# First batch's partial sums between two feed-forward turns: from DRAM to SBUF, with the second turn's inputs in the activations' ring

## The chip, the cores and the metric

The kernel runs on one core of a Trainium2 chip. The metric is the device time of one execution in microseconds (us). Engines are named as in the profile: PE (matrix products) with its weight loads PEld, DVE (vector), ACT (scalar), POOL (GpSimd), and SP, which here only issues DMAs, in order, each after its waits.

## The reference

```
x    = concat_heads(softmax(mask(q k^T / 8)) v)   # 8 batches, 8 heads, 576 tokens, 64 wide; mask by blocks of 64
h    = (x^T @ U @ V)^T                            # mixes the tokens, rank 32
u    = x + h                                      # [8, 576, 512]
out  = u + max(u @ w_ch1, 0) @ w_ch2              # 512 -> 2048 -> 512
```

All arrays are float32; `U`, `V`, `w_ch1` and `w_ch2` are float64 and are turned into float32 pairs on the chip.

## The kernel before, in words

The work is written as tasks, each with an engine, an estimated duration, a priority, the buffers that it reads, writes or only holds, and a delay until a DMA lands. `Plan.issue` then plays the tasks through with these estimates and issues on each engine the ready task with the lowest priority number. That game fixes the order of the instructions on every engine before the kernel is built; on the chip each engine keeps to its order and waits where an operand is late. A change of a task's waits or of its place moves the order of everything that the game comes to afterwards. In that game two tasks that use the SBUF port which DVE and POOL share (flag `port`, and every POOL task) never run together.

Attention goes head by head (64 heads, priorities 0 to 64,000). For each head: q and k are split into a high and a low part (POOL lines 894, 895), copied into the lower 64 partitions by two DMAs (lines 897, 898, `q<-q`, `k<-k`), multiplied (PE lines 944, or 948 and 949), reduced to a maximum (DVE 962), exponentiated (ACT 973), normalised (DVE 989, 990; POOL 999), transposed (PE 1032; its copies are ACT 1009 and DVE 1051 into `ph`, `pl`) and applied to v (PE 1091). `mix` (1116 to 1160) makes the input u of the feed-forward part and stores it in DRAM (`u_d`).

The feed-forward part fills PE's gaps: its products have priorities of 1e6 and more. The first 1024 of the 2048 hidden units are done by `ffn_chunk`, for 16 chunks of 288 tokens (two for each batch). One chunk: u is loaded into `ur` (two sets of four tiles, chunk c uses set c mod 2), split into `uh` (ACT 445) and `ul` (POOL 447, four instructions in a row), multiplied by the first weights into a PSUM bank (PE 465), read out with a maximum against zero into `hh` (ACT 470) and its rest `hl` (DVE 473), multiplied by the second weights (PE 488), added to u (DVE 494, into `ot`) and stored (SP 499, into `o_d`). All this has two PSUM banks, `banks_f` (`bf_90`, `bf_91`). `hh` and `hl` are rings of 10 tiles, taken in turn by `take`.

While the weights of the first half still arrive (their pieces pass through `st` and `z`: SP 372 and 387, ACT 353 and 360, DVE 331, 332, 337, 345, POOL 361), the two chunks of batch 0 are done in two turns: turn 0 with hidden units 0 to 511, turn 1 with 512 to 1023.

```
    for n in range(2):
        for c in range(CPB):
            ffn_chunk(c, lambda: wa, wab, range(n * FH, (n + 1) * FH), n)
    for c in range(CPB, NCHUNK):
        ffn_chunk(c, lambda: wa, wab)
```

Before, turn 0 stores u plus its products in `o_d`; turn 1 loads u from `u_d` again, splits it, and then loads the sums from `o_d` over it (SP 452). The last 1024 hidden units follow as block products of seven instead of eight (PE 659), after attention has ended.

Of the kernel before, what the change touches and what calls it, by code (L numbers as in the profile page):

```python
# [24 lines left out]
KC = DM // P  # L25
FC = HF // P
T = 288
# [26 lines left out]
NEAR, DL = 130, 3000  # L54
# [83 lines left out]
class Plan:  # L138
# [8 lines left out]
    def add(self, engine, ns, prio, fn, reads=(), writes=(), hold=(), after=0, port=False):  # L147

        n = len(self.tasks)
        deps = set()  # L150
        for b in reads:
            deps.update(b.writers)
            b.readers.append(n)
        for b in hold:
            deps.update(b.readers, b.writers)
        for b in writes:
            deps.update(b.readers, b.writers)
            b.writers, b.readers = [n], []
        deps.discard(n)
        slots = {b for b in (*reads, *writes) if b.pool is not None}  # L160
        for b in slots:
            b.users += 1
        self.tasks.append((engine, ns, prio, fn, deps, after, slots, port or engine == "POOL"))
# [76 lines left out]
def _act(n, sbuf=False):  # L240
    return (93 if sbuf else 52) + 0.833 * n


def _dve(n):
    return 69 + 1.042 * n


def _pe(*ns, m=()):

    m = [*m, *[P] * len(ns)][1 : len(ns)] + [P]  # L250
    return sum(max(0.85 * w, n * COL) for n, w in zip(ns, m))
# [3 lines left out]
def attention_then_mixer(  # L255
# [10 lines left out]
    nc = tc.nc  # L266
# [8 lines left out]
    add = plan.add  # L275

    def f32(ap):
        return ap.bitcast(F32)
# [15 lines left out]
    u_d = [dram.tile([P, KC, S], F32, name=f"u_d{b}") for b in range(B)]  # L294
    o_d = [dram.tile([P, KC, S], F32, name=f"o_d{b}") for b in range(B)]
    u_s = [[Buf().split(CPB) for _ in range(NPAIR)] for _ in range(B)]
    o_s = [[Buf() for _ in range(KC)] for _ in range(NCHUNK)]
# [10 lines left out]
    def take(r, name):  # L308
        n = used[name] = used.get(name, -1) + 1
        return r[n % len(r)]  # L310
# [112 lines left out]
    hh_r, hl_r = ([Buf() for _ in range(FC + 2)] for _ in range(2))  # L423
    ot_t = fp.tile([P, 3, T], F32, name="ot")
    ot_r = [Buf(ot_t[:, n, :]) for n in range(3)]
# [5 lines left out]
    def ffn_chunk(c, w, wb, fr=range(FC), turn=0):  # L431

        b, o = c // CPB, (c % CPB) * T
        banks, done = banks_f if c < NCHUNK - 1 else Part(banks_f, banks_f), ffn_done[c]
        E, F = -1.0, 1e6 + (1300 + 300 * c if turn else 1000 * c)
        ur = ur_r[c % 2]
        for k in range(KC):
            if b > 0 or turn:
                add(
                    "SP", 630, E, lambda k=k: nc.sync.dma_start(out=ur[k].ap, in_=u_d[b][:, k, o : o + T]),  # L440
                    u_s[b][k].parts, [ur[k]], after=DL,
                )
        for k in range(KC):
            uh, ul = uh_r[k], ul_r[k]
            add("ACT", _act(T, True), E, lambda u=ur[k], h=uh: nc.scalar.copy(h.ap, u.ap), [ur[k]], [uh])
            add(
                "POOL", 780, E, lambda u=ur[k], h=uh, l=ul: nc.gpsimd.tensor_sub(l.ap, u.ap, f32(h.ap)),  # L447
                [ur[k], uh], [ul],
            )
            if turn:  # L450
                add(
                    "SP", 630, E, lambda k=k: nc.sync.dma_start(out=ur[k].ap, in_=o_d[b][:, k, o : o + T]),
                    [o_s[c][k]], [ur[k]], after=DL,
                )
        hs = {}
        for f in fr:
            ps = Buf(pool=banks)
            fs = slice(f * P, (f + 1) * P)
            ops = [(wn, k, m) for wn, m in (("w1h", uh_r), ("w1l", uh_r), ("w1h", ul_r)) for k in range(KC)]
            for g in range(0, len(ops), GM):  # L460

                def products(g=g, ps=ps, fs=fs, ops=ops):
                    for i in range(g, g + GM):
                        wn, k, m = ops[i]
                        nc.tensor.matmul(ps[:, :T], w()[wn][:, k, fs], m[k].ap, start=(i == 0), stop=(i == len(ops) - 1))  # L465

                sub = ops[g : g + GM]
                add("PE", _pe(*[T] * GM), F, products, [m[k] for _, k, m in sub] + [wb["w1"][f * P // CW][k] for _, k, _ in sub], [ps])
            th, tl = take(hh_r, "hh"), take(hl_r, "hl")
            add("ACT", _act(T), E, lambda ps=ps, th=th: nc.scalar.activation(th.ap, ps[:, :T], AF.Relu), [ps], [th])  # L470
            add(
                "DVE", _dve(T), E,
                lambda ps=ps, th=th, tl=tl: nc.vector.scalar_tensor_tensor(  # L473
                    out=tl.ap, in0=ps[:, :T], scalar=0.0, in1=f32(th.ap), op0=ALU.max, op1=ALU.subtract
                ),
                [ps, th], [tl],
            )
            hs[f] = (th, tl)
        for m in range(KC):
            ps = Buf(pool=banks)  # L480
            ms = slice(m * P, (m + 1) * P)
            ops = [(wn, f, x) for f in fr for wn, x in (("w2h", 0), ("w2l", 0), ("w2h", 1))]
            for g in range(0, len(ops), GM):

                def products(g=g, ps=ps, ms=ms, ops=ops):
                    for i in range(g, g + GM):
                        wn, f, x = ops[i]
                        nc.tensor.matmul(ps[:, :T], w()[wn][:, f, ms], hs[f][x].ap, start=(i == 0), stop=(i == len(ops) - 1))  # L488

                sub = ops[g : g + GM]  # L490
                add("PE", _pe(*[T] * GM), F, products, [hs[f][x] for _, f, x in sub] + [wb["w2"][f] for _, f, _ in sub], [ps])
            ot = take(ot_r, "ot")
            add(
                "DVE", _dve(T), E, lambda ps=ps, ot=ot, m=m: nc.vector.tensor_add(ot.ap, ps[:, :T], ur[m].ap),
                [ps, ur[m]], [ot],
            )
            done.writers.append(len(plan.tasks) - 1)
            add(
                "SP", 630, E, lambda ot=ot, m=m: nc.sync.dma_start(out=o_d[b][:, m, o : o + T], in_=ot.ap), [ot],
                [o_s[c][m]], after=DL,  # L500
            )
# [308 lines left out]
    for r in raw_r:  # L810
# [3 lines left out]
        for x, fill in ((qi, 1.0), (ki, NEG)):  # L814
            nc.gpsimd.affine_select(
                out=x[:, :, 1, :], in_=x[:, :, 1, :], pattern=[[-1, 4], [0, 64]], compare_op=ALU.not_equal,
# [390 lines left out]
# [5 lines that stand above are left out]
# [40 lines left out]
```

## Time and profile before

| | |
|---|---|
| time, median of 3 runs | 1182.98 us (1182.54 to 1184.93) |
| the profiled execution's own time | 1186.81 us |
| its span in the profile | 1185.0 us |
| PE busy | 1165.8 us, 98% |
| DVE, ACT, POOL busy | 937.3, 775.9, 451.3 us |
| DMA | 122.69 MB, mean 104 GB/s |
| mean granted TensorE clock | 0.998 |

The span runs from the first to the last recorded instruction. PE has the same matrix products to do in any order, so its idle time and the time at a lowered clock are what an order can win or lose.

### The profile page before, as it was taken

The page shows a single profiled execution, that of the slowest core. Times are in us where ns is not written, and L with a number is a line of the kernel's source. Part 1 is how long each engine was busy: PE and PEld are TensorE (multiplying, and loading weights), DVE is VectorE, ACT ScalarE, POOL GpSimd, SP SyncE. Part 2 cuts the span into 40 slices and gives each one's busy share as a digit, 9 for nine tenths or more (in the row PEclk, how much of TensorE's full clock was granted, in tenths as well). Part 3 has the DMA queues.
Part 4 walks back from the last instruction along what each step waited for, and adds up shares of the span by engine and source line. Part 5 has one row for each costly group of instructions (what it writes and reads, how often), then busy time and mean ns, then how long its engine had stood idle before and what let it go on. Part 6 is the DMA issues. An engine that isn't in the chain of part 4 may idle for free.

```text
span 1185.0 us, 25201 instructions
## 1 busy us (share of the span) xinstructions
PE 1165.8 (98%) x8988; PEld 1133.4 (96%) x8988; DVE 937.3 (79%) x2008; ACT 775.9 (65%) x1924; POOL 451.3 (38%) x582
## 2 busy tenths in 40 slices
PE   9989899999999999999999999999999999999998
PEld 7778899999999999999999999999999999999998
DVE  6898888877787878787877587326989889889887
ACT  7888787889888888898887342114544444444443
POOL 5656767576767676766674112110000000000000
PEclk9999999999999999999999999999999999999999
DMA  5455555444434434444331434211232132142121
GB/s 139 146 150 154 136 170 151 118 120 112 115 112 113 112 105 112 121 113 106 110 102 51 138 115 133 75 50 52 61 121 65 57 120 70 52 121 66 56 81 41
DMA packets 75868, 122.69 MB, mean 104 GB/s; under 512 B 8928, under 2 KB 52960, under 8 KB 75744
## 3 DMA queue, kind: packets, MB, share of 16 engines
q1 hardware_dynamic: 75744, 121.09, 35.6%
q8 instruction: 71, 1.16, 0.4%
q14 instruction: 53, 0.43, 0.1%
HBM read 76.23 MB, written 29.49 MB: 89 GB/s over the span
## 4 chain that ended last, share of the span: by engine, by line
PE 77%; DVE 10%; ACT 8%; issue 3%; DMA 2%; SPq 0%; POOL 0%; ACTq 0%; DVEq 0%; POOLq 0%
PE bb L659 30%; PE bf L465 10%; PE bf L488 10%; PE ba L1032 6%; PE ba L1091 5%; PE bg L488 4%; PE bg L465 4%; ACT p L973 3%; DVE mx L962 2%; PE ba L949 2%; PE ba L948 2%; DVE pl L1051 1%; PE bw L948 1%; ACT ph L1009 1%; PE ba L1116 1%
## 5 line engine op out<-in xcount | busy, mean ns | idle before, releaser
L999 POOL TENSOR_SCALAR p<-p,rv 128x192 f32<-128x192 f32 (+4 forms) x320 | 172.1, 553 | 157.6 <-DVE rv L990 84.5
L659 PE MATMUL bb<-hh,w1l 128*128 128x288 f32 x704 | 170.1, 295 | 0.0
L659 PE MATMUL bb<-hh,w1h 128*128 128x288 f32 x704 | 169.4, 295 | 0.0
L1051 DVE TENSOR_TENSOR pl<-ba,ph 128x512 fp32r<-128x512 f32 x216 | 113.8, 551 | 18.3 <-ACT ph L1009 16.0
L973 ACT ACTIVATE p<-ba,mx 128x448 f32<-128x448 f32 (+2 forms) x248 | 115.0, 466 | 15.4 <-DVE mx L962 11.8
L1032 PE MATMUL ba<-ident,p 128*128 128x128 f32 x768 | 123.0, 275 | 2.0 <-POOL p L999 0.7
L659 PE MATMUL bb<-hl,w1h 128*128 128x288 f32 x576 | 123.0, 295 | 0.1
L659 PEld LDWEIGHTS bb<-hh,w1l 128*128 128x128 f32 x704 | 123.0, 190 | 0.0
L659 PEld LDWEIGHTS bb<-hh,w1h 128*128 128x128 f32 x704 | 121.9, 188 | 0.0
L488 PE MATMUL bf<-hh,w2h 128*128 128x288 f32 x384 | 119.0, 310 | 2.3 <-DVE hl L473 2.3
L488 PE MATMUL bf<-hl,w2h 128*128 128x288 f32 x384 | 113.8, 296 | 0.0
L488 PE MATMUL bf<-hh,w2l 128*128 128x288 f32 x384 | 113.0, 294 | 0.0
L447 POOL TENSOR_TENSOR ul<-ur,uh 128x288 fp32r<-128x288 f32 x72 | 61.6, 884 | 127.1 <-PE bf L465 80.8
L1009 ACT CAST ph<-ba 128x512 fp32r<-128x512 f32 x216 | 99.0, 492 | 10.8 <-PE ba L1032 9.6
L613 ACT CAST hh<-hb 128x576 fp32r<-128x576 f32 x98 | 65.9, 672 | 60.5 <-PE bb L659 59.3
L962 DVE TENSOR_REDUCE mx<-ba 128x1 f32<-128x448 f32 (+3 forms) x248 | 95.2, 406 | 11.2 <-PE ba L949 8.6
L1032 PEld LDWEIGHTS ba<-ident,p 128*128 128x128 f32 x768 | 90.0, 141 | 7.5 <-POOL p L999 2.7
L659 PEld LDWEIGHTS bb<-hl,w1h 128*128 128x128 f32 x576 | 91.9, 188 | 0.4 <-DVE hl L614 0.4
L1091 PE MATMUL ba<-ph,vs 128*128 128x256 f32 (+3 forms) x432 | 90.4, 263 | 0.0
L465 PE MATMUL bf<-uh,w1l 128*128 128x288 f32 x392 | 82.1, 305 | 0.0
L894 POOL TENSOR_TENSOR q<-raw,q 64x576 fp32r<-64x576 f32 x52 | 73.8, 1419 | 7.7 <-issue 5.4
L895 POOL TENSOR_TENSOR k<-raw,k 64x576 fp32r<-64x576 f32 x52 | 75.1, 1445 | 2.2 <-POOL p L999 0.5
(172 smaller groups left out, 3363.4 us busy)
## 6 DMA issues: line engine op xcount, KB each, us to landing
raw<-in_qk_dram SPq DMA_DIRECT2D x63, 288.0 KB, 3.9
st<-in_w_dram SPq DMA_DIRECT2D x32, 512.0 KB, 4.1
o_d<-ot SPq DMA_DIRECT2D x72, 144.0 KB, 1.8
vr<-in_v_dram SPq DMA_DIRECT2D x32, 320.0 KB, 3.7
ur<-u_d SPq DMA_DIRECT2D x64, 144.0 KB, 2.5
whole<-o_d SPq DMA_DIRECT2D x32, 288.0 KB, 3.2
out_dram<-whole SPq DMA_DIRECT2D x32, 288.0 KB, 2.2
ur<-u_d SPq DMA_DIRECT2D x30, 288.0 KB, 3.2
```

What stands on the lines that cost most here:

```text
L465: nc.tensor.matmul(ps[:, :T], w()[wn][:, k, fs], m[k].ap, start=(i == 0), stop=(i == len(ops) - 1))
L488: nc.tensor.matmul(ps[:, :T], w()[wn][:, f, ms], hs[f][x].ap, start=(i == 0), stop=(i == len(ops) - 1))
L659: nc.tensor.matmul(bank[:, i, :T], x()[:, w(k)], p.ap[:, k, :], start=first and n == 0, stop=last and n == len(ops) - 1)
L894: add("POOL", 1380, pr, lambda: nc.gpsimd.tensor_sub(q1[top], raw[top, 0:S], f32(q2[top])), [raw, q2], [q1])
L895: add("POOL", 1380, pr, lambda: nc.gpsimd.tensor_sub(k2[top], raw[top, S : 2 * S], f32(k1[top])), [raw, k1], [k2])
L962: lambda i=i, at=at: nc.vector.tensor_reduce(out=mx[: P if i else 64, i : i + 1], in_=view(i, at), op=ALU.max, axis=AX.XY if wide else AX. ...
L973: nc.scalar.activation(out.rearrange("p (j k) -> p j k", j=2) if wide else out, view(i, at), AF.Exp, bias=mx[:rows, i : i + 1], accum_out= ...
L999: lambda x=x, rows=rows, i=i: nc.gpsimd.tensor_scalar(out=x, in0=x, scalar1=rv[:rows, i : i + 1], scalar2=1.0, op0=ALU.mult, op1=ALU.mult),
L1009: add("ACT", _act(n), pr, lambda: nc.scalar.copy(out(), inp()), reads, writes)
L1032: nc.tensor.transpose(out=bank[:, a : a + P], in_=pt_r[i][h % PB[i]][:, j * P : (j + 1) * P], identity=perm.ap)
L1051: "DVE", _dve(m), pr, lambda: nc.vector.tensor_sub(pl[:, low], bank[:, :m], f32(ph[:, low])), [bank, bh], [bl]
L1091: nc.tensor.matmul(bank[0 : c.stop, a:n], vs[:, j, c], x[:, _at(g, j)], start=(i == 0), stop=(i == len(ops) - 1))
```

## The change

Turn 0's sums are added into `ur` itself and stay there; nothing goes to `o_d`. Turn 1 takes four tiles of the `hh` ring for its inputs, loads u into them (as bits of the same size), splits from there, adds its products to `ur`, and stores the end sums as before. So eight stores (`o_d<-ot`) and eight loads (`ur<-o_d`) of 144 KB go; the eight loads of u in turn 1 stay, with another target and other waits. Eight tiles more are taken from the ring of `hh`, none from that of `hl`.

```
         ur = ur_r[c % 2]
+
+        us = [take(hh_r, "hh") for _ in range(KC)] if turn else ur
         for k in range(KC):
+            u, at = us[k], (lambda u=us[k]: f32(u.ap) if turn else u.ap)
             if b > 0 or turn:
                 add(
-                    "SP", 630, E, lambda k=k: nc.sync.dma_start(out=ur[k].ap, in_=u_d[b][:, k, o : o + T]),
-                    u_s[b][k].parts, [ur[k]], after=DL,
+                    "SP", 630, E, lambda k=k, at=at: nc.sync.dma_start(out=at(), in_=u_d[b][:, k, o : o + T]),
+                    u_s[b][k].parts, [u], after=DL,
                 )
-        for k in range(KC):
             uh, ul = uh_r[k], ul_r[k]
-            add("ACT", _act(T, True), E, lambda u=ur[k], h=uh: nc.scalar.copy(h.ap, u.ap), [ur[k]], [uh])
-            add(
-                "POOL", 780, E, lambda u=ur[k], h=uh, l=ul: nc.gpsimd.tensor_sub(l.ap, u.ap, f32(h.ap)),
-                [ur[k], uh], [ul],
-            )
-            if turn:
-                add(
-                    "SP", 630, E, lambda k=k: nc.sync.dma_start(out=ur[k].ap, in_=o_d[b][:, k, o : o + T]),
-                    [o_s[c][k]], [ur[k]], after=DL,
-                )
+            add("ACT", _act(T, True), E, lambda at=at, h=uh: nc.scalar.copy(h.ap, at()), [u], [uh])
+            add(
+                "POOL", 780, E, lambda at=at, h=uh, l=ul: nc.gpsimd.tensor_sub(l.ap, at(), f32(h.ap)), [u, uh], [ul],
+            )
...
-            ot = take(ot_r, "ot")
+            ot = ur[m] if len(fr) < FC and not turn else take(ot_r, "ot")
...
+            if ot is ur[m]:
+                continue
```

The order changes from early in turn 0 on. Three places, which the prediction calls A, B and C; line numbers after the change are lower by two to four behind the edit (465, 473, 488, 494 are 461, 469, 484, 490).

**Place A, end of turn 0's first layer for chunk 0.** On PE, before, two products of `mix` stand between the last first-layer product (into `bf_91`) and the first second-layer product:

```order
L465 MATMUL bf_91<-ul_113,w1h_212 128x288
L1145 MATMUL ba_96<-v_183,t_0_178 128x288
L1145 MATMUL ba_97<-v_183,t_0_178 128x288
L488 MATMUL bf_90<-hh,w2h_214 128x288
L488 MATMUL bf_90<-hh,w2l_215 128x288
L488 MATMUL bf_90<-hl,w2h_214 128x288
```

On PE after the change, at the same place:

```order
L461 MATMUL bf_91<-ul_113,w1h_212 128x288
L484 MATMUL bf_90<-hh,w2h_214 128x288
L484 MATMUL bf_90<-hh,w2l_215 128x288
L484 MATMUL bf_90<-hl,w2h_214 128x288
L484 MATMUL bf_90<-hh,w2h_214 128x288
L484 MATMUL bf_90<-hh,w2l_215 128x288
L484 MATMUL bf_90<-hl,w2h_214 128x288
L484 MATMUL bf_91<-hh,w2h_214 128x288
```

The two products of `mix` have moved behind twelve second-layer products, and six of these write `bf_91` right behind the six on `bf_90`. On DVE, before, the reading out of the two banks (`hl`) at the same place:

```order
L1136 TENSOR_TENSOR t_0_178<-tz_179,t_0_178 32x128
L989 TENSOR_REDUCE rv_167<-ss_144 128x2
L990 RECIPROCAL rv_167<-rv_167 128x2
L337 SCALAR_TENSOR_TENSOR z_102<-st_100,z_102 128x512
L473 SCALAR_TENSOR_TENSOR hl<-bf_90,hh 128x288
L345 SCALAR_TENSOR_TENSOR z_102<-st_100,z_102 128x512
L1150 TENSOR_TENSOR ut_181<-ba_96,xt_174 128x288
L473 SCALAR_TENSOR_TENSOR hl<-bf_91,hh 128x288
```

On DVE after the change:

```order
L987 TENSOR_REDUCE rv_167<-ss_144 128x2
L988 RECIPROCAL rv_167<-rv_167 128x2
L469 SCALAR_TENSOR_TENSOR hl<-bf_90,hh 128x288
L987 TENSOR_REDUCE rv_167<-ss_144 128x3
L988 RECIPROCAL rv_167<-rv_167 128x3
L1134 TENSOR_TENSOR t_0_178<-tz_179,t_0_178 32x128
L345 SCALAR_TENSOR_TENSOR z_102<-st_100,z_102 128x512
L469 SCALAR_TENSOR_TENSOR hl<-bf_91,hh 128x288
```

Line 345, a piece of the weights, still stands ahead of the second `hl`, and now a second pair of `rv` and line 1136's successor (1134) do as well.

**Place B, the DMAs of the next two heads on SP.** Before, with the stores and loads of turn 0's end among them:

```order
L897 DMA q_1_157<-q_1_138 64x576
L499 DMA o_d_82<-ot 128x288
L440 DMA ur_104<-u_d_74 128x288
L898 DMA k_1_159<-k_1_159 64x576
L499 DMA o_d_82<-ot 128x288
L440 DMA ur_104<-u_d_74 128x288
L868 DMA raw_142<-in_qk_dram 64x1152
L387 DMA st_101<-in_w_dram 128x1024
L897 DMA q_0_156<-q_0_137 64x576
L898 DMA k_0_158<-k_0_158 64x576
```

On SP after the change, for the same two heads:

```order
L387 DMA st_101<-in_w_dram 128x1024
L443 DMA hh<-u_d_74 128x288 x2
L895 DMA q_1_157<-q_1_138 64x576
L896 DMA k_1_159<-k_1_159 64x576
L866 DMA raw_142<-in_qk_dram 64x1152
L895 DMA q_0_156<-q_0_137 64x576
L896 DMA k_0_158<-k_0_158 64x576
```

The weights' piece `st_101` now goes ahead of both heads' copies, no store or load of sums is left, and two loads into the `hh` ring stand where they were (two more stand eleven rows earlier).

**Place C, end of turn 0's first layer for chunk 1.** On DVE before:

```order
L337 SCALAR_TENSOR_TENSOR z_102<-st_100,z_102 128x512
L473 SCALAR_TENSOR_TENSOR hl<-bf_90,hh 128x288
L1150 TENSOR_TENSOR ut_181<-ba_97,xt_175 128x288
L1051 TENSOR_TENSOR pl_171<-ba_95,ph_169 128x512
L1150 TENSOR_TENSOR ut_181<-ba_97,xt_175 128x288
L345 SCALAR_TENSOR_TENSOR z_102<-st_100,z_102 128x512
L473 SCALAR_TENSOR_TENSOR hl<-bf_91,hh 128x288
```

On DVE after the change:

```order
L469 SCALAR_TENSOR_TENSOR hl<-bf_90,hh 128x288
L337 SCALAR_TENSOR_TENSOR z_102<-st_100,z_102 128x512
L331 TENSOR_SCALAR z_103<-z_103 128x512
L332 TENSOR_SCALAR z_103<-z_103 128x512
L469 SCALAR_TENSOR_TENSOR hl<-bf_91,hh 128x288
L1148 TENSOR_TENSOR ut_181<-ba_98,xt_175 128x288
L1148 TENSOR_TENSOR ut_181<-ba_97,xt_175 128x288
L987 TENSOR_REDUCE rv_167<-ss_144 128x3
L988 RECIPROCAL rv_167<-rv_167 128x3
L345 SCALAR_TENSOR_TENSOR z_102<-st_100,z_102 128x512
L337 SCALAR_TENSOR_TENSOR z_103<-st_101,z_103 128x512
```

The second `hl` now stands five rows ahead of line 345 instead of right behind it.

## Rows read from the trace of the kernel before

**Rows 1.** The page: busy time, share of the span and instructions of each engine.
```profile
PE 1165.8 (98%) x8988; PEld 1133.4 (96%) x8988; DVE 937.3 (79%) x2008; ACT 775.9 (65%) x1924; POOL 451.3 (38%) x582
```
**Rows 2.** Busy time by stretch of the span, us; granted clock, DMA share, GB/s.
```profile
0.00:110.00 110.00, 101.81 (x605) 83.50 (x606) 91.58 (x234) 90.83 (x251) 62.84 (x91) 1.00 0.50 145
...
120.00:135.00 15.00, 13.85 (x118) 13.42 (x117) 12.67 (x30) 11.63 (x32) 11.29 (x13) 1.00 0.79 191
135.00:143.00 8.00, 6.82 (x51) 6.67 (x52) 6.67 (x18) 7.08 (x21) 5.16 (x8) 1.00 0.08 20
143.00:155.00 12.00, 9.65 (x67) 9.40 (x66) 8.47 (x17) 6.64 (x20) 8.61 (x9) 0.86 0.59 183
155.00:180.00 25.00, 25.00 (x206) 24.63 (x205) 22.22 (x56) 20.95 (x57) 19.09 (x26) 1.00 0.57 166
180.00:300.00 120.00, 119.55 (x989) 116.11 (x988) 95.09 (x259) 106.16 (x299) 81.02 (x105) 1.00 0.44 121
300.00:660.00 360.00, 358.19 (x2967) 349.53 (x2966) 279.46 (x751) 308.56 (x871) 234.46 (x306) 1.00 0.38 104
660.00:1140.00 480.00, 479.87 (x3614) 479.63 (x3614) 377.08 (x573) 197.71 (x327) 20.31 (x21) 1.00 0.29 87
1140.00:1185.00 45.00, 41.01 (x309) 40.77 (x308) 34.39 (x50) 16.48 (x26) 0.00 (x0) 1.00 0.11 38
```
**Rows 3.** PE's waits, whole span: us in total, times, longest.
```profile
PE bf L488 <- DVE hl L473: 2.3, 1, 2.3
...
PE bw L948 <- DMA k<-k: 1.6, 1, 1.6
...
PE ba L1032 <- DVE pl L1051: 0.7, 1, 0.7
```
**Rows 4.** PE's instructions in time, 113 to 137 us: start, duration, idle before.
```profile
113.64 0.30 PE L488 MATMUL bf<-hh,w2h 128*128 128x288 f32 x1
...
134.14 0.40 PE L1130 MATMUL ba<-xl,ust 128*64 128x128 f32 x4
136.18 0.37 PE L948 MATMUL bw<-k,q 128*128 128x288 f32 x1 [1.64 <-DMA k<-k]
```
**Rows 5.** The chain that ended last, one piece: start, us, what.
```profile
150.80 0.80 PE bf L488 x6
```
**Rows 6.** DVE's instructions in time at places A and C.
```profile
113.22 0.87 DVE L345 SCALAR_TENSOR_TENSOR z<-st,z 128x512 int32<-128x512 int32 x1
...
114.38 0.44 DVE L473 SCALAR_TENSOR_TENSOR hl<-bf,hh 128x288 fp32r<-128x288 f32 x1
...
142.51 3.17 DVE L345 SCALAR_TENSOR_TENSOR z<-st,z 128x512 int32<-128x512 int32 x1
145.61 0.44 DVE L473 SCALAR_TENSOR_TENSOR hl<-bf,hh 128x288 fp32r<-128x288 f32 x1
```
**Rows 7.** POOL's instructions in time at the same two places.
```profile
113.68 3.37 POOL L447 TENSOR_TENSOR ul<-ur,uh 128x288 fp32r<-128x288 f32 x4
...
141.44 1.43 POOL L894 TENSOR_TENSOR q<-raw,q 64x576 fp32r<-64x576 f32 x1
142.83 3.52 POOL L447 TENSOR_TENSOR ul<-ur,uh 128x288 fp32r<-128x288 f32 x4
```
**Rows 8.** SP's DMA issues in time, place B.
```profile
124.87 0.32 SPq L499 DMA_DIRECT2D o_d<-ot  x1
...
126.68 0.95 SPq L387 DMA_DIRECT2D st<-in_w_dram  x1
...
128.28 0.55 SPq L898 DMA_DIRECT2D k<-k  x1
```
**Rows 9.** The tile k between 100 and 190 us: seven DMAs' time to landing.
```profile
DMA to landing us min/median/max: 2.3/3.5/7.8
```
**Rows 10.** The page's DMA issues: KB each, median us to landing.
```profile
o_d<-ot SPq DMA_DIRECT2D x72, 144.0 KB, 1.8
...
ur<-o_d SPq DMA_DIRECT2D x8, 144.0 KB, 2.8
```

## The prediction

> **What bounds the kernel now.** I read the page first, then PE's busy time by stretch, then PE's waits, and then the timelines of PE, DVE, POOL and SP around the stretches that lose time. PE is busy for 1165.8 us of a span of 1185.0 [rows 1], so 19.2 us are idle, and the change adds or removes no matrix product. The stretches say where those 19.2 us lie [rows 2]: 8.2 before 110 us, where attention has no feed-forward products to fill gaps with yet; 1.15 in 120 to 135, 1.18 in 135 to 143 and 2.35 in 143 to 155; nothing in 155 to 180; 0.45 in 180 to 300, 1.81 in 300 to 660, 0.13 in 660 to 1140, and 4.0 at the end. The change first moves an instruction that matters at about 113 us. The early 8.2 and the last 4.0 us are therefore out of its reach, and so is the stretch behind 660, where PE never waits. What it can win is the loss in 120 to 155 us, 4.7 us idle, and a lowered clock: in the 12 us from 143 on the granted clock averages 0.86, part of it at 1.2 instead of 2.4 GHz, right behind the longest idle piece, which is worth (1 - 0.86) x 12 = 1.7 us. Together 6.4 us. The stretches from 155 to 660, 2.26 us idle, can go either way.
>
> Three waits make up nearly all of the 4.7 us [rows 3]. First, 0.7 us for `pl`, at 121 us. Second, 1.64 us for a DMA `k<-k`: PE finishes its last product at 134.5 and goes on at 136.18 [rows 4], the DMA was issued at 128.28 [rows 8] and took 7.8 us, the longest of seven whose median is 3.5 [rows 9]. Third, 2.35 us for `hl`: the DVE instruction of line 345 ahead of it took 3.17 us at 142.51, against 0.87 at 113.22 [rows 6], while POOL ran a `q` and then four `ul` without a gap [rows 7].
>
> **What goes.** Sixteen transfers of 144 KB (eight of `o_d<-ot`, eight of `ur<-o_d`) [rows 10]. By themselves they cost PE nothing before: they run on SP and the DMA engines, and no wait of PE is for either of them [rows 3]. What they cost is room ahead of others. At place B four such stores stand in SP's queue, each behind an addition on DVE; the last went at 124.87, and `q`, `k` and `raw` of the next heads stand behind it, so that `k_0` went at 128.28 [rows 8], into DMA engines that were 79% busy from 120 to 135 [rows 2]. In the new order seven rows stand from `st_101` to `k_0`, with none of these stores. The two loads into the ring that replace them wait for PE's reading of two `hh` tiles in the last part of turn 0's second layer, about where the last store waited. `k_0` then follows five issues later, each about 0.5 us, at some 126 to 127 us. The wait of 1.64 falls to between 0 and all of it; I take 1.2 us gained, nearer to all, since 1.5 us of earlier issue and 0.6 MB less in the queues point the same way. For the 0.7 us of `pl`, lines 331, 332 and 337 of a weights' piece no longer stand between `hl` and `pl`: between 0 and 0.7, I take 0.5.
>
> At place C the second `hl` moves ahead of line 345, so a long line 345 can't hold it. The gain is 2.35 us, and with the idle piece gone the 1.7 us of low clock behind it; lines 337, 331 and 332 of the weights stand ahead of it now, but they should run before the four `ul` start. Gains so far: 2.35 + 1.7 + 1.2 + 0.5 = 5.75 us.
>
> **What comes in.** At place A the two products of `mix` no longer cover the reading out of `bf_91`. Before, PE began the second layer at 113.64 [rows 4], 0.3 us after its first-layer products; now it begins there at about 113.4, and six products take 0.80 us [rows 5], so it wants `bf_91` at 114.2. The `hl` that frees that bank ended at 114.38 + 0.44 = 114.82 [rows 6], with a line 345 of 0.87 us. So PE idles at least 0.6 us. Line 345 now also stands behind a pair of `rv` that waits for exponentials, and so falls into the four `ul` that POOL starts at 113.68 [rows 7]. If it loses one of these, 3.37 / 4 = 0.84 us, the idle time is 1.4; if it loses as much as at 142.51, 3.17 - 0.87 = 2.3 us, it is 2.9. I take 1.4: line 345's two rows lie at both ends, and the middle case is one `ul`.
>
> Here the Trainium skill has a rule (SBUF — State Buffer, section "SBUF: two separate sides"): DVE and GpSimd share one pair of ports by an exclusive lock, and the one that comes second waits for the whole instruction of the first. By it place A would cost 0.6 + 0.84 = 1.4 us at the most, the value taken. The trace has a worse case: line 345 came at 142.51, the `q` ended at 142.87, and yet it ended only at 145.68 [rows 6, 7], so it let more than one of POOL's instructions pass. With the 2.9 us of that row in place of 1.4 the sum below would be 1.5 us higher.
>
> Behind the second `hl` at place C stand lines 345 and 337, both against POOL's `ul`, and behind them the additions that free the two banks. PE has 24 second-layer products (4 x 0.80 = 3.2 us [rows 5]) before it needs a bank from them, so a loss of 2.3 us is mostly covered: between 0 and 2.3, I take 0.8. Turn 1's loads into the ring wait for readers, but they did so for `ur` too, and `uh` of turn 1 waits for the first layer of chunk 1 on PE in either order; hidden behind these products, no cost. If that cover went, a load costs its landing, 2.8 us [rows 10].
>
> Everything behind 155 us is reordered too, with the same work. Its 2.26 us idle over 505 us could be 0 or could double (between -2.3 and +2.3); since it is far below the rate ahead of it, I add 1.0.
>
> **The sum.** -5.75 + 1.4 + 0.8 + 1.0 = -2.55 us. On the profiled execution's own time of 1186.81 (1.8 beside its span) that is 1184.3. That execution lies 3.8 us above the median of the runs, with the same order of work; on the median, 1182.98 - 2.55 = 1180.4 us. About 0.2%, 2.4 us, is what a measurement of this kernel can tell from no change, so this forecast lies just beyond it.
>
> **The rivals.**
> - *The stall only moves.* Line 345 loses to the `ul` at place A as it did at C, 2.9 us instead of 1.4, and the clock falls again behind it, 1.7 us. Sum -5.75 + 2.9 + 1.7 + 0.8 + 1.0 = +0.65: 1183.6 us, no change. For it: it stands before `hl` at A in the new order, with the four `ul` on POOL at the same time. Against it: at A before, with nearly the same neighbours, it took 0.87 us.
> - *The old stalls all go and nothing comes.* Gains of the upper ends, 2.35 + 1.7 + 1.64 + 0.7 = 6.4, less the 0.6 us at A that the bank costs anyway: 1177.2 us. For it: 155 to 180, with turn 1 in it, was free of idle time. Against it: three more port instructions in a row than before.
> - *The ring starves the filler: slower.* Turn 1's inputs hold four of ten `hh` tiles until POOL has split them, and its third and fourth hidden tiles are those that chunk 1's second layer reads last. If the first layer then has no tile to be read out into, PE has attention alone, and idles at the rate of the first 110 us, 8.2 / 110 = 0.074 us per us [rows 2], or more as weights pile up. Over the 67 us in which the turns run, 113 to 180, that is 5.0 us, with the 1.7 us of clock that an idle piece cost before: 1180.4 + 6.7 = 1187.1 us. It decides from 5.0 us on, where the sum passes +2.4. Against it: PE's new order has the second layer of chunk 1 ahead of the products that need those tiles.
> - *Hidden anyway.* The transfers were covered, and the three waits come back under other names: 1183 us.
>
> **How the numbers follow.** Chances: forecast 0.45, the stall only moves 0.24, all go 0.13, the starved ring 0.10, hidden anyway 0.08. The likeliest's own range is 1178.5 to 1182.3 (place A from 0.6 to 2.9, the rest behind 155 from 0 to +2). The range over all reaches from the case in which all goes, 1177.2, to 1185.0, which takes in the moved stall with a spread of runs of 1.4 us, and leaves out most of the starved ring. Of the forecast about 0.32 lies beyond 0.2%; faster 0.32 + 0.13 + 0.02 = 0.47. Slower: the starved ring and 0.07 of the moved stall with a worse order behind 155, 0.17. Within 0.2%: 0.36.
>
> **What the profile after would show.** Right: no 3 us line 345 directly ahead of an `hl` that PE waits for at place C, PE idle in 135 to 155 us under 1 us, clock 1.00 there, `k<-k` landing in time, an idle piece of 1 to 2 us near 114 us with `hl` as its releaser, and some 2.5 to 3.5 us less idle time and low clock in all before 180 us. Wrong: an idle piece of 3 us at 114 to 118 us with a low clock behind it, waits for DMA on `q` or `k` that were not there, or idle time behind 180 us of 4 us or more.

## The result: slower by 0.3%, and the profile after

The changed kernel took 1187.67 us (median of 17 runs, 1184.60 to 1189.72) against 1183.35 us before (17 runs, 1182.48 to 1186.47). The ratio is 1.0030, with a 95% interval of 1.0022 to 1.0039: slower by 4.3 us, outside the forecast range (1177.2 to 1185.0 us). The profiled execution took 1186.39 us, its span is 1184.6 us. The profiled execution of the kernel before took 1186.81 us, so these two executions alone would show no loss: the one before lies 3.8 us above the median then known, the one after 1.3 us below its median. The page's first line of the changed kernel is close to that of [rows 1]:

```profile
PE 1164.1 (98%) x8988; PEld 1132.8 (96%) x8988; DVE 937.2 (79%) x2008; ACT 775.3 (65%) x1924; POOL 452.3 (38%) x582
```

The work is the same, so I look again for where PE stands still and where its clock is low. PE's busy time by stretch of the changed kernel, from 110 to 660 us, in the stretches of [rows 2] and one more, 110 to 120 us:

```profile
110.00:120.00 10.00, 8.01 (x49) 7.67 (x48) 8.44 (x20) 7.47 (x21) 8.76 (x12) 0.87 0.55 156
120.00:135.00 15.00, 15.00 (x124) 14.95 (x123) 11.50 (x28) 11.58 (x30) 10.44 (x12) 0.97 0.51 135
135.00:143.00 8.00, 7.86 (x64) 7.51 (x63) 7.75 (x21) 7.86 (x23) 3.98 (x6) 1.00 0.15 44
143.00:155.00 12.00, 11.36 (x93) 11.34 (x94) 10.17 (x27) 9.87 (x28) 10.06 (x13) 1.00 0.62 172
155.00:180.00 25.00, 24.03 (x195) 22.97 (x194) 22.02 (x54) 21.10 (x58) 20.43 (x25) 1.00 0.40 105
180.00:300.00 120.00, 119.33 (x985) 116.03 (x984) 92.58 (x253) 102.52 (x292) 78.86 (x102) 1.00 0.43 119
300.00:660.00 360.00, 356.78 (x2965) 349.07 (x2964) 279.23 (x752) 308.55 (x873) 236.23 (x308) 1.00 0.38 105
```

Idle in 120 to 155 us fell from 4.7 to 0.8 us, as forecast. But 1.99 us appeared in 110 to 120, 0.97 in 155 to 180 and 3.89 in 180 to 660, where before it was 0, 0 and 2.26.

**Place A.** PE's, DVE's and POOL's instructions in time (start, duration, engine, line, idle before in brackets):

```profile
116.12 0.40 PE L484 MATMUL bf<-hh,w2h 128*128 128x288 f32 x1 [1.99 <-DVE hl L469]
```
```profile
113.64 0.85 DVE L1134 TENSOR_TENSOR t<-tz,t 32x128 fp32r<-32x128 f32 x1
114.50 1.19 DVE L345 SCALAR_TENSOR_TENSOR z<-st,z 128x512 int32<-128x512 int32 x1
115.61 0.45 DVE L469 SCALAR_TENSOR_TENSOR hl<-bf,hh 128x288 fp32r<-128x288 f32 x1
```
```profile
113.53 3.76 POOL L449 TENSOR_TENSOR ul<-ur,uh 128x288 fp32r<-128x288 f32 x4 [0.57 <-ACT uh L447]
```

PE waits 1.99 us for the second `hl`, which stands behind `t` and line 345, and both run against four `ul` on POOL. Line 345 took 1.19 us against 0.87 in [rows 6] and a median of 0.67 over the whole kernel, and `t` took 0.85 us against a median of 0.28. By the Trainium skill (SBUF — State Buffer, section "SBUF: two separate sides") a DVE instruction with two inputs in SBUF that comes second to a GpSimd instruction that reads SBUF waits until that one has ended. That is up to 3.76 / 4 = 0.94 us here, and what `t` (0.57 us) and line 345 (0.52 us against its median) lost is within it. Behind the idle piece PE's clock fell to its lower level, 1.2 GHz, for a while. The same view as above, in stretches of 2 us:

```profile
116.00:118.00 2.00, 1.88 (x12) 1.89 (x13) 1.97 (x5) 1.97 (x4) 2.00 (x3) 0.83 0.63 188
118.00:120.00 2.00, 2.00 (x9) 1.97 (x9) 1.63 (x4) 0.21 (x1) 2.00 (x5) 0.50 0.56 221
120.00:122.00 2.00, 2.00 (x14) 1.95 (x13) 1.64 (x3) 0.62 (x2) 2.00 (x2) 0.81 0.00 0
```

That is 2 x (0.17 + 0.50 + 0.19) = 1.7 us lost. This is what the rival "the stall only moves" names, with 2.0 us of idle time where it has 2.9. It doesn't explain the slower result yet: that rival's sum was 1183.6 us.

### The profile page after: what moved, and what is told of

The parts are those of the page before. It is cut to its first block, busy times and chain, and to the rows that moved or that the text cites. A ratio compares the mean times of both kernels' runs of the same rounds, so it can differ in the third digit from the quotient of the medians.

```text
span 1184.6 us, 25144 instructions
## 1 busy us (share of the span) xinstructions
PE 1164.1 (98%) x8988; PEld 1132.8 (96%) x8988; DVE 937.2 (79%) x2008; ACT 775.3 (65%) x1924; POOL 452.3 (38%) x582
## 4 chain that ended last, share of the span: by engine, by line
PE 77%; DVE 9%; ACT 8%; issue 2%; DMA 2%; POOL 1%; SPq 0%; ACTq 0%; DVEq 0%; POOLq 0%
PE bb L657 30%; PE bf L484 10%; PE bf L461 10%; PE ba L1030 6%; PE ba L1089 5%; PE bg L461 4%; PE bg L484 4%; ACT p L971 3%; DVE mx L960 2%; PE ba L947 2%; PE ba L946 1%; DVE pl L1049 1%; PE ba L1128 1%; ACT ph L1007 1%; PE ba L1114 1%
## 5 line engine op out<-in xcount | busy, mean ns | idle before, releaser
L484 PE MATMUL bf<-hh,w2h 128*128 128x288 f32 x392 | 122.6, 313 | 3.3 <-DVE hl L469 3.2
L484 PE MATMUL bf<-hh,w2l 128*128 128x288 f32 x392 | 115.4, 294 | 0.0
L449 POOL TENSOR_TENSOR ul<-ur,uh 128x288 fp32r<-128x288 f32 x64 | 55.8, 899 | 118.1 <-PE bf L461 54.9
L1089 PE MATMUL ba<-ph,vs 128*128 128x256 f32 (+3 forms) x432 | 88.0, 260 | 0.0
L484 PEld LDWEIGHTS bf<-hh,w2h 128*128 128x128 f32 x392 | 74.1, 189 | 4.7 <-DVE hl L469 4.1
```

The lines of the kernel that those rows point to most:

```text
L1089: nc.tensor.matmul(bank[0 : c.stop, a:n], vs[:, j, c], x[:, _at(g, j)], start=(i == 0), stop=(i == len(ops) - 1))
```

## The experiments

Every ratio below is to the kernel before, run on the same chip in turn. Line numbers of e1, e5, f2 and f4 are higher than those of the change by 18 (484 is 502), those of e7, e11 and e12 by 1.

| run | what it is | median us | ratio, 95% interval |
|---|---|---|---|
| e1 | change, A mended | 1186.20 | 1.0023 (1.0015 to 1.0031) |
| e2 | order of before, no transfers | 1183.40 | 1.0000 (0.9991 to 1.0009) |
| e3 | before, other order behind 180 us | 1182.94 | 0.9994 (0.9986 to 1.0003) |
| e4 | before, one profiled execution | 1182.71 | |
| e5 | change, A mended, other order behind 180 us | 1184.06 | 0.9998 (0.9988 to 1.0008) |
| e6 | change, other order from some 108 us | 1187.81 | 1.0036 (1.0022 to 1.0049) |
| e7 | change, own input tiles, other order from some 70 us | 1183.65 | 0.9999 (0.9990 to 1.0009) |
| e8 | change, one profiled execution | 1185.09 | |
| e9 | change, other order behind 180 us | 1183.72 | 0.9995 (0.9984 to 1.0006) |
| e10 | change, other order from some 107 us | 1184.22 | 1.0001 (0.9991 to 1.0010) |
| e11 | own input tiles, other order from some 70 us | 1187.82 | 1.0020 (1.0010 to 1.0030) |
| e12 | own input tiles, other order from some 106 us | 1190.07 | 1.0041 (1.0025 to 1.0056) |

**e1: place A mended.** One row of DVE moves, nothing else:

```diff
 L988 RECIPROCAL rv_167<-rv_167 128x3
+L469 SCALAR_TENSOR_TENSOR hl<-bf_91,hh 128x288
 L1134 TENSOR_TENSOR t_0_178<-tz_179,t_0_178 32x128
 L345 SCALAR_TENSOR_TENSOR z_102<-st_100,z_102 128x512
-L469 SCALAR_TENSOR_TENSOR hl<-bf_91,hh 128x288
```

> The changed kernel with one edit: at place A the second hl goes ahead of the two DVE instructions (the mix part t and the weights' line 345) that stood directly before it; every other engine keeps its order word for word. Theory (the moved stall at A is paid in every run): PE's wait of 1.99 us for hl at 114 us shrinks to under 0.9 us, the stretch at 1.2 GHz behind it (117.4 to 120.7 us, 1.7 us lost) goes, and the median falls by 2.5 to 3.5 us to about 1184.5. Rival (the loss is spread over the reordered stretch behind 155 us and A is not paid in the median run): the median stays within 1 us of 1187.7.

The wait at A shrank from 1.99 to 0.52 us, but the median still lies 0.23% above before, and neither the theory (2.5 to 3.5 us less) nor the rival (within 1 us) was met: it came down by 1.5 us. Most of the loss is not at A.

**e2: no transfers, the order of before.** The plan is that of before, so every compute instruction stands where it stood; only the transfers of the sums are empty, turn 0's sums go to `ur`, and turn 1's inputs have four tiles `ui` of their own:

```diff
-lambda k=k: nc.sync.dma_start(out=ur[k].ap, in_=o_d[b][:, k, o : o + T]),
+lambda: None,
...
-nc.vector.tensor_add(ot.ap, ps[:, :T], ur[m].ap),
+nc.vector.tensor_add(to.ap, ps[:, :T], ur[m].ap),
```

> The kernel before with the change's data flow but its own order: sums stay in ur, the sixteen transfers are gone, turn 1's inputs go into four tiles of their own, and PE, DVE, ACT and POOL keep the order of before word for word. Theory (the order costs, the transfers were hidden): 1183.4 plus or minus 1 us, the same as before. Rival (the transfers' room matters, the k wait of 1.6 us goes): 1181.5 us or less.

No difference within the interval of 0.1%. The sixteen transfers of 144 KB were hidden before; taking them away gains nothing by itself. In its profile the copies of `k` do land sooner, within 4.2 us between 100 and 190 us, against 7.8 at the most in [rows 9] (5.9 in e3, 6.6 in e4).

**e3 and e4: another order of before, and before once more.** e3 gives the planner another estimate for batch 0's `o_d` stores, which leaves the order alone up to some 180 us and changes it behind:

```diff
-"SP", 630, E,
+"SP", 1000 if c < CPB else 630, E,
```

> The kernel before with only the planner's estimate for the stores of batch 0's chunks changed (630 to 1000 ns): the same instructions and transfers, in the order of before up to about 180 us on PE and in another order behind. Theory (any other order behind 155 us costs some 2 us, since the order of before is a lucky one there): 1185 us or more. Rival (the order behind makes no difference on the whole): 1183.4 plus or minus 1 us.

> The kernel before once more, for a second profile. Theory (the profile that the prediction used was an unlucky execution, 3.5 us above the median of 17 runs): its time is nearer to 1183.4, and the 3.2 us line 345 at place C, the idle piece of 2.35 us and the low clock behind it are absent or much smaller. Rival (these stalls are in every execution): all three are there again.

e3 shows that a reorder need not cost; its theory (1185 us or more) failed. e4 upsets the base of the prediction. Busy time by stretch in this second execution of the kernel before, to be held against [rows 2]:

```profile
120.00:135.00 15.00, 13.96 (x119) 13.56 (x118) 12.67 (x31) 11.62 (x31) 11.29 (x13) 1.00 0.75 191
135.00:143.00 8.00, 7.15 (x55) 6.65 (x53) 7.79 (x18) 7.90 (x25) 6.38 (x9) 1.00 0.17 55
143.00:155.00 12.00, 12.00 (x100) 11.78 (x101) 9.27 (x24) 8.66 (x24) 10.78 (x13) 1.00 0.76 223
155.00:180.00 25.00, 24.91 (x202) 24.13 (x201) 23.12 (x57) 19.74 (x55) 18.25 (x22) 1.00 0.61 176
180.00:300.00 120.00, 119.50 (x989) 116.06 (x987) 94.78 (x258) 107.45 (x303) 81.26 (x105) 1.00 0.42 115
300.00:660.00 360.00, 358.25 (x2966) 349.76 (x2965) 276.92 (x746) 304.21 (x860) 231.90 (x303) 1.00 0.38 104
```

In 120 to 155 us 1.9 us are idle, not 4.7, and the clock is 1.00 throughout. PE's waits there, and two of DVE's instructions at place C, in e4:

```profile
PE bf L488 <- DVE hl L473: 0.8, 1, 0.8
PE ba L1032 <- DVE pl L1051: 0.7, 1, 0.7
PE bw L948 <- issue: 0.3, 1, 0.3
```
```profile
140.82 1.67 DVE L345 SCALAR_TENSOR_TENSOR z<-st,z 128x512 int32<-128x512 int32 x1
142.41 0.45 DVE L473 SCALAR_TENSOR_TENSOR hl<-bf,hh 128x288 fp32r<-128x288 f32 x1
```

The same order, and line 345 takes 1.67 us instead of 3.17; PE stands 0.3 us ahead of the products on `k` instead of 1.6. Of the 6.4 us that the change "could win", 4.5 us belonged to one execution. The profiles of e2 and e3 have the same order up to some 180 us, and both bear e4 out, with 1.8 and 1.9 us idle in 120 to 155 us at full clock and 1.67 us for line 345 at place C:

```profile
120.00:155.00 35.00, 33.16 (x270) 32.08 (x268) 29.79 (x69) 28.22 (x78) 28.50 (x33) 1.00 0.44 124
```
```profile
120.00:155.00 35.00, 33.13 (x271) 32.02 (x269) 29.74 (x70) 28.48 (x79) 28.46 (x34) 1.00 0.59 166
```

**e5 to e8: the ring, or the order?** The change also put inputs and hidden rows into one ring. e5 keeps the ring, mends A, and takes e3's estimate (1000 ns); e6 keeps the ring with another estimate for turn 1's loads; e7 gives the inputs four tiles of their own in the plan:

```diff
-"SP", 630, E, lambda k=k, at=at:
+"SP", 700 if turn else 630, E, lambda k=k, at=at:
```
```diff
-us = [take(hh_r, "hh") for _ in range(KC)] if turn else ur
+us = ui_r if turn else ur
```

> The changed kernel with two edits of order alone: at place A the second hl ahead of t and L345 (as in e1), and behind some 180 us another order of everything, got by giving the planner 1000 ns instead of 630 ns for batch 0's o_d stores (the same figure that reordered the kernel before in e3). Buffers and data flow are those of the change. Theory O (the rest of the loss, some 3 us of idle TensorE behind 155 us, is this one order's luck): the idle between 155 and 660 us falls from 4.9 to 5.8 us to about 3, and the median to 1182.5 to 1184.5. Theory R (inputs and hidden rows now share one ring of ten, so filler comes late in whatever order): idle stays near 5 us and the median at 1185.5 to 1187.

> The changed kernel with 700 ns instead of 630 ns as the planner's estimate of the second turn's loads of inputs, which reorders everything from some 110 us on; at place A the mix products stand ahead of the F2 group again and L345 still ahead of the second hl. Theory O: no half clock behind place A and another idle sum behind 155 us, 2 to 5 us; the median 1182.5 to 1186, apart from e5's and from the change's own 1187.7 by more than the interval. Theory R: idle behind 155 us near 5 us, the median 1185.5 to 1187.5.

> The changed kernel, but the second turn's inputs go into four tiles of their own and not into the activations' ring; sums stay in SBUF as in the change. The planner then makes yet another order, from some 95 us on. Theory R (the shared ring is the cost): idle behind 155 us falls to about 2 to 3 us and the median to 1182 to 1184.5, whatever the order. Theory O (the order is the cost): this order is one more draw, anywhere between 1182 and 1188, and its time follows its idle TensorE time behind 110 us.

> The changed kernel once more, one look. Theory of the order: the wait of F2 for the second hl at place A is there again (1.5 to 2.5 us) with a half clock behind it in some executions, and the idle time between 155 and 660 us is 4 to 6 us. If it is only an unlucky execution, as the profiled one of the kernel before was, idle there is 2 to 3 us.

e5, with the ring, is level with before; so is e7, without it, but in another order. e6 takes as long as the change, above what either theory gave, with another wait (2.0 us for `xl` at 162 us). e8 repeats the profile of the change: 1.99 us idle at A, this time at full clock, and 4.9 us idle in 155 to 660. Those waits belong to the order; the low clock behind A comes in some executions only.

**e9 to e12: more orders.** e9 is the change with 1000 ns alone. e10 has the ring with 900 ns for turn 1's loads; e11 and e12 have own tiles with 700 and 400 ns.

> The changed kernel with e5's other order behind some 180 us, and place A left as the change has it (F2 waits for the second hl). So far: the change 1187.7, with A mended 1186.2 (e1), with A mended and the other order behind 180 us 1184.1 (e5). Theory O, two separate prices that add up: 1187.7 less some 2.1 us for the order behind 180 us, 1185 to 1186. If the price of A shows only together with the order behind it, or the other way round: about 1184 or about 1187.7.

> The changed kernel, inputs in the activations' ring, with 900 ns for the second turn's loads: one more order, other from some 110 us on. Three orders with the ring so far gave 1187.7, 1184.1 and 1187.8, three without it 1183.2, 1182.9 and 1183.7. Theory O (each order its own draw, ring or not): anywhere from 1182.5 to 1188. Theory R in its weaker form (the ring lets good orders be, but makes most of them some 3 us worse): 1185 to 1188.

> The second turn's inputs in four tiles of their own (as e7), with 700 ns for their loads: another order from some 85 us on. Theory O: anywhere from 1182.5 to 1188, and its time follows the idle TensorE time between 110 and 660 us of its profile (4.2 us at 1183, 7.7 at 1187). Theory R, weaker form: 1182.5 to 1184.5 like the other orders without the ring.

> The second turn's inputs in four tiles of their own (as e7), with 400 ns for their loads: another order again, from some 95 us on. Theory O: anywhere from 1182.5 to 1188. Theory R, weaker form: 1182.5 to 1184.5. If e11 and e12 both stay under 1184.5 and e10 comes out above 1185, the ring is likely part of the cause; if one of the two comes out above 1185.5, it is not needed for it.

The ring is not needed for the loss: e11 and e12 are slower without it, e10 and e9 are level with it. e11's loss is nearly all clock: span times mean granted clock, the span as it would be at full clock, averages 1182.0 us (1181.4 in the kernel before beside it), and the low clock takes 3.7 us of a span (1.3 before). e12, slower than any theory had it, has 1185.4 and 2.6 us. What e12 lost at full clock stands in a new place. PE's waits of e12, 143 to 180 us:

```profile
PE ba L1031 <- DVE pl L1050: 1.9, 1, 1.9
PE ba L1031 <- DVE ut L1149: 1.6, 1, 1.6
PE ba L1031 <- DVE ph L1057: 1.0, 1, 1.0
```

And e9 surprised: it leaves A as the change has it, and is level with before, not at the 1185 to 1186 us of two prices that add up. Either A costs nothing, or e9 was flattered. Four kernels on one chip were to settle it.

**f1 to f4: A and the order behind 180 us, on one chip.** f1 is the change, f2 is e1, f3 is e9, f4 is e5.

> First of four kernels on one chip: the changed kernel as it is. If the loss of 4.3 us is the kernel's and not a chip's: ratio to before 1.002 to 1.004, about 1187 us, some 1.5 us a run lost to half clocks and some 1184 us without them (span times granted clock).

> Second of four: place A mended alone (the second hl first, as e1). If A carries a part of the loss: 1 to 2 us under f1. If A carries none by itself (as e9 against e5 says): within 0.7 us of f1.

> Third of four: the other order behind 180 us alone, A as in the change (as e9). From a mix product near 170 us, with the same work before it, the profiled executions needed 1015.4 us to the end in the change (twice the same) and 1013.1 us in e9. If that order is the main part: 2 to 4 us under f1, and the profile shows 1013 us again. If e9 was flattered by its chip: under 1.5 us below f1.

> Fourth of four: both edits (as e5). If the two prices add: f2 plus f3 less f1, some 1182 to 1184. If the mend of A gives nothing behind the other order: f3 within 0.7 us.

| | median us | ratio, 95% interval | span x granted clock, mean | span x (1 - clock), mean |
|---|---|---|---|---|
| before (29 runs) | 1183.95 | | 1180.8 | 1.4 |
| f1, the change (9) | 1187.29 | 1.0029 (1.0019 to 1.0040) | 1183.5 | 1.7 |
| f2, A mended (8) | 1186.35 | 1.0023 (1.0010 to 1.0035) | 1183.5 | 1.0 |
| f3, other order (11) | 1184.39 | 1.0007 (0.9995 to 1.0018) | 1181.0 | 1.8 |
| f4, both (11) | 1183.96 | 1.0001 (0.9992 to 1.0011) | 1180.9 | 1.2 |

The last two columns split each execution's span by its mean granted clock, and average over the runs: what it would be at full clock, and what the low clock took. Each mean of f1 to f4 has a standard error of 0.2 to 0.5 us (the scatter of the runs over the root of their number). The first column has two levels only, 1183.5 with the change's order behind 180 us and 1181.0 with the other; the mend of A does not move it. So the order behind 180 us carries 2.5 us, clear of the scatter. The second falls by 0.7 us with the mend in both pairs, which neither pair alone can tell from nothing; by medians the mend gives 0.9 and 0.4 us, inside the intervals, and f2's 0.9 us lies between what was expected if A carries a part (1 to 2 us) and if it carries none (under 0.7 us).

The profiles point the same way, though they are few. PE from 110 to 135 us in f1, e9, e8 and f3, which all have A as in the change:

```profile
110.00:135.00 25.00, 22.02 (x158) 20.99 (x158) 19.91 (x46) 18.13 (x49) 17.43 (x21) 0.93 0.47 132
```
```profile
110.00:135.00 25.00, 22.01 (x159) 21.14 (x158) 19.83 (x46) 18.25 (x49) 17.47 (x21) 0.93 0.49 131
```
```profile
110.00:135.00 25.00, 23.01 (x184) 22.50 (x183) 21.61 (x51) 20.59 (x55) 20.18 (x23) 1.00 0.55 151
```
```profile
110.00:135.00 25.00, 23.01 (x188) 22.58 (x187) 21.57 (x50) 20.59 (x55) 19.85 (x23) 1.00 0.56 155
```

With the change's first profile, the clock fell behind A in three of five executions, for 1.7 us each; with A mended (e1, e5, f2, f4) it is 1.00 there in all four. A price of A of some 0.7 us, all of it clock, fits, but is not shown beyond the scatter.

That the 2.5 us lie behind 180 us is seen in single profiles too. The last product of `mix` before 180 us has the same work before it in f1 and f3. Its time (first and last start) in f1 and in f3:

```profile
core 0 of [0], span 1186.4 us
...
L1143 PE MATMUL ba<-v,t x2: 292/332/373, 170.5 to 170.9; 96*128 96x288 f32 x2
```
```profile
core 0 of [0], span 1180.8 us
...
L1143 PE MATMUL ba<-v,t x2: 293/332/370, 167.2 to 167.6; 96*128 96x288 f32 x2
```

From there to the end: 1186.4 - 170.9 = 1015.5 and 1180.8 - 167.6 = 1013.2 us. What comes before varies by 3.0 us between executions of one order (the product starts at 169.2 us in the change's first profile, 170.9 in f1 and 167.9 in e8). What comes behind repeats to 0.2 us: 1015.4 in the change's first profile and e8 and 1015.5 in f2; 1013.1 in e9 and 1013.0 in e5 and f4. Only e1's profile, 1016.4, lies off. PE's largest waits in 155 to 660 us in the change:

```profile
PE ba L1143 <- DVE xt L1097: 1.0, 3, 0.6
PE ba L1143 <- ACT p L971: 0.8, 3, 0.3
PE ba L1030 <- DVE ph L1056: 0.7, 3, 0.2
PE bf L484 <- DVE hl L469: 0.5, 1, 0.5
```

and in f3:

```profile
PE ba L1030 <- ACT p L971: 1.5, 3, 0.6
PE bf L484 <- DVE hl L469: 0.5, 1, 0.5
```

The products of `mix` no longer wait in f3, but for 0.2 us at 167 us, ahead of the other order. The stretches in f3, against 119.33 and 356.78 us busy in the change:

```profile
180.00:300.00 120.00, 119.16 (x992) 117.51 (x991) 92.62 (x249) 102.06 (x289) 79.53 (x103) 1.00 0.41 113
300.00:660.00 360.00, 358.13 (x2970) 349.94 (x2969) 277.65 (x752) 309.31 (x869) 235.00 (x306) 1.00 0.38 106
```

That is 2.7 us idle instead of 3.9, so 1.2 of the 2.3 us is idle time of PE. The other 1.1 us shows as busy time: from that `mix` product to the end PE counts as busy for 1006.7 us in f1 and 1005.7 in f3, with the same number of products. All of the 2.3 us lies ahead of the block products of the last 1024 hidden units, whose first group in f1 and f3 is

```profile
L657 PE MATMUL bb<-hh,w1h x704: 290/296/299, 825.4 to 1172.3; 128*128 128x288 f32 x176
```
```profile
L657 PE MATMUL bb<-hh,w1h x704: 290/296/299, 819.7 to 1166.6; 128*128 128x288 f32 x176
```

so that both need 361 us from its start to the end. Which of the moved rows between 180 and 820 us cost the time was not tried.

That the mend of A saves no time at full clock is seen in f4 against f3, at A in f4:

```profile
114.61 0.40 PE L502 MATMUL bf<-hh,w2h 128*128 128x288 f32 x1 [0.52 <-DVE hl L487]
...
118.58 0.36 PE L964 MATMUL ba<-k,q 128*128 128x192 f32 x1 [0.62 <-DVE ut L1166]
```

Of the 1.5 us won, 0.6 comes back 4 us later as a wait for `ut`, which stands behind the rows that `hl` passed, and the last `mix` product before 180 us starts at 167.7 us in f4 and 167.6 in f3, both at full clock. That attention's chain through DVE and ACT sets the pace there, and not PE, would fit; it was not tried.

## Why the prediction was wrong

**The step that failed: "What it can win is the loss in 120 to 155 us".** The three waits and the low clock there were read from one execution, 3.8 us longer than the median, priced at 5.75 us, and then taken off the median. But most of them were what made that execution long. In e4, near the median, the stretch has 1.9 us idle at full clock (e2 and e3: 1.8 and 1.9); the change leaves 0.8. The gain was 1.1 us, not 5.75. By its terms: `pl` 0.7 us (0.5 forecast), `k` 0.3 (1.2 forecast), and at place C nothing for `hl` and the clock behind it (2.35 + 1.7 forecast), since PE waits there for 0.8 us in e4 and as long after the change. With 1.1 us and the other terms as they stood (1.4 + 0.8 + 1.0), the sum would have been +2.1 us, 1185.1 us: this one step turns the sign of the forecast.

**The term for the order behind 155 us was mis-sized.** "Everything behind 155 us is reordered too ... I add 1.0", with bounds of 2.3. Between the two executions at full clock, e4 and e8, idle time in 155 to 180 us rose by 0.9 us (0.1 to 1.0) and in 180 to 660 by 1.7 (2.2 to 3.9): 2.6 us. (The spans of the two differ by 2.4 us, 1180.9 and 1183.3, and all idle time from 110 to 660 us by 3.5, so idle time overstates the loss, as at A.) By f1 against f3 the order behind 180 us alone carries 2.5 us. It is no property of the change: e5, e9 and f4 have the same data flow and are level with before. f3 also tells what is left: with the other order behind 180 us the change lies 0.2 us above before at full clock and 0.4 us in the clock's share, both within the scatter, so all that it moves ahead of 180 us, gains and place A together, comes to about nothing.

**Place A: the wait was right, its worth was not.** Idle 2.0 us against 1.4 forecast, in the bounds of 0.6 to 2.9, with `hl` as its releaser, and 1.98 or 1.99 in all five profiles of it. It includes a loss of 0.57 us of `t`, which stands ahead of `hl` in the new order and which the prediction did not price; with one POOL instruction of 0.84 us for each of `t` and line 345, 0.6 + 2 x 0.84 = 2.3 us would have covered it. But for the mend, which closes 1.5 us of it, the runs give 0.7 us of clock, not clear of the scatter, and nothing at full clock: the prediction took idle PE time for lost time in a stretch where it comes back. The 0.8 us for the banks behind place C did not come: in 120 to 155 us PE waits for `hl` alone.

**Places B and C: the order did what was said, and gained little.** Time to landing of `k` between 100 and 190 us, and PE at place C, in the change:

```profile
DMA to landing us min/median/max: 3.2/4.1/5.5
```
```profile
143.64 0.40 PE L484 MATMUL bf<-hh,w2h 128*128 128x288 f32 x1 [0.78 <-DVE hl L469]
```
```profile
143.14 0.45 DVE L469 SCALAR_TENSOR_TENSOR hl<-bf,hh 128x288 fp32r<-128x288 f32 x1
144.51 0.69 DVE L345 SCALAR_TENSOR_TENSOR z<-st,z 128x512 int32<-128x512 int32 x1
```

PE no longer waits for `k`, which lands within 5.5 us against 7.8 at the most in [rows 9]. But in e4 it lands within 6.6 us, and that cost PE no more than 0.3. Line 345, now behind the second `hl`, can't delay it. The 0.78 us that PE still waits there is what the kernel before has in its usual execution too (0.8 us in e4), with line 345 at 1.67 us ahead of `hl`.

**The rivals.** "Hidden anyway" was right about the transfers (e2). "The stall only moves" was right in kind about place A (2.0 us, not 2.9, and the low clock in three of five profiles), and short by the order behind. "The ring starves the filler" named nearly the time that came (1187.1 us) by luck, for a reason that e10, e9 and f4 exclude: they have the ring and are level with before.

**A bound that does not follow.** The likeliest case's own range is given as 1178.5 to 1182.3 us. From its two terms, place A (0.6 to 2.9 instead of 1.4) and the rest behind 155 us (0 to 2 instead of 1.0), it is 1178.6 to 1182.9. The result lies far outside either.

## What to carry to other kernels

Where one execution's time lies above the median of the runs, its largest waits are the first suspects for the difference: look at a second execution before a gain is priced on them. Where a planner makes the order, any edit of a cost or a buffer draws a new order: here eleven orders of the same products lay between 0.06% faster and 0.41% slower, so time the edit in several of them, or with the old order kept (as e2), before the edit gets the blame or the credit. A gap of PE need not be lost time: the mend of A closed 1.5 us of one, and the product at 167 us came no earlier.

## What the runs showed of the hardware

- One order of instructions on one core varies by 5.7 us from execution to execution (1181.95 to 1187.69 us for the kernel before, beside f1 to f4). The mean granted clock goes with it: of the 29 runs beside e9 to e12, spans averaged 1181.5 us at a mean granted clock of 1.0 (11 runs), 1182.3 at 0.999 (7), 1183.6 at 0.998 (8) and 1185.7 at 0.997 (3).
- The same idle piece of 1.99 us at place A was followed by a stretch at 1.2 GHz in the change's first profile (granted clock 0.50 in 118 to 120 us) and not in e8, the same kernel, whose clock is 1.00 from 110 to 135 us in the row above.
- The Trainium skill (TensorE: Matmul & The Clock Gate, section "Part 1: The HAM clock gate (the "warmup" mystery)") says that how many products run at the low clock at a kernel's start varies from run to run of one kernel. These two profiles show such a difference behind an idle piece in mid-kernel, which the page's sentence does not speak of; at a kernel's start no run here was read for it.
- Line 345 on a tile of 128x512, each time beside POOL's `ul`, took 0.69, 0.87, 1.19, 1.67 and 3.17 us in the places and executions shown. At one place it repeats: 1.19 us in all five profiles with A as in the change. At place C of the order before it took 1.67 us in e2, e3 and e4 and 3.17 in the first profile. At place C of the change, 0.69 us is no more than its median over the kernel (0.67), though POOL ran four `ul` from 142.06 to 145.86 us.
